# The first 512 tokens by two transposing loads instead of turns on TensorE

## The chip, the cores and the metric

One core of one Trainium2 chip runs the kernel. The metric is the device time of one execution in microseconds (us). A profiled execution gives, beside its own time, the trace that the views below are taken from; times inside it count from the start of its span.

## The reference

The input x has 2048 tokens of 512 numbers in bfloat16. Two branches are computed from it and mixed token by token with a gate:

```python
def reference(A_x, A_wqkv, A_w_phi, A_wo, B_x, B_w1, B_w2, gate_w):
    x = A_x
    g = _sigmoid((x * gate_w).sum(-1, keepdims=True))
    a = _A_ref(x, A_wqkv, A_w_phi, A_wo)   # linear attention, 32 heads of 16
    b = _B_ref(x, B_w1, B_w2)              # relu(x @ w1) @ w2, 1376 hidden
    return g * a + (1 - g) * b
```

In the attention branch q and k of each head go through w_phi (16 x 16), then softmax of the result and of its negative give 32 features; keys and values are summed into one 32 x 16 matrix per head, the queries are multiplied with it and divided by their sum, and wo closes it. B_x is not used.

## The kernel before

Every operation is a named task in a graph with its engine and its dependencies. The order of each engine's tasks is written out by hand in the table ORDER (L17 to L62): one string each for SyncE (`sp`), GpSimd (`pool`), ScalarE (`act`), VectorE (`dve`) and TensorE (`pe`). `emit` puts the tasks on the engine in that order, with a wait for each dependency on another engine or on a load, so an engine stands still when its next task's wait is not over. The numbers `dur`, `lat` and `boost` of a task do not reach the program.

The products need x with its 512 features on the partitions, in the buffer XT: four blocks of 128 features, 2048 tokens wide. x comes in four chunks of 512 tokens. Chunks 1 to 3 (`x1`, `x2`, `x3`) and the weights of K and Q (`wkT`, `wqT`) are loaded by transposing DMAs of SyncE's queue, all issued at L277. Chunk 0 goes another way. Four plain loads of 128 tokens (`x00` to `x03`, L272) bring it into XN, which lies in a buffer of FT; TensorE multiplies each block of 128 x 128 with an identity, IDN, (`xt00` to `xt31`, L350, 16 matmuls), and ScalarE (`xe*0`, L362) and VectorE (`xe*1`, L365) copy the results from PSUM to XT. IDN is made on VectorE (L320) from two iotas of GpSimd.

W1 (512 x 1376) is loaded in parts: its first 512 columns as four blocks of 128 rows (`w1a0` to `w1a3`, alternately on SyncE's and ScalarE's queue), then columns 512 to 1023 (`w1b`) and the rest (`w1c`). Tasks `h{c}_{k}` compute tile k of 128 hidden columns for chunk c, in four matmuls of 512 columns (L391). For chunk 0 the first four tiles are cut up: `hh00`, `hh01`, `hh1`, `hh2`, `hh3` (L405) do the first 256 tokens, W1's row block by row block into four PSUM banks, and `hr0`, `hr1`, `h0_0` to `h0_3` (L411) the other 256 tokens. `h0_4` is the first task at L391. Next come `h0_5`, then the folds `f1_0` to `f1_3` (L374), which multiply K's transposed weights with w_phi (block-diagonal in WBD, made by VectorE from the load `wphi`), and the K projections `pr_k0` on (L512). In front of all is `warm0` (L258): matmuls of 512 columns on constants of one, whose result is not used.

The x turns and the first products stand in the order "warm0 xt00 xt01 xt10 xt11 hh00 hh01 hh1 hh2 xt20 xt21 xt30 xt31 hh3 hr0 hr1 h0_0 ..." on TensorE. SyncE begins with "x00 w1a0 w1a2 x02 x03 w1b wphi wkT w1c wv x1 x2 wqT x3" and ScalarE with "x01 w1a1 w1a3 xe00 xe10 xe20 xe30 rl0_0"; `x1` waits on SyncE for `w1c` to land. `rl{c}_{k}` are ScalarE's relu copies (L469).

Later stages: softmax on ScalarE, VectorE and GpSimd (L539 to L589), the sum over keys (L573), the queries (L616 to L625), W2 and wo (L638, L644), and the stores.

Of the kernel before, what the change touches and what calls it, by code (L numbers as in the profile page):

```python
# [18 lines left out]
        "x00 w1a0 w1a2 x02 x03 w1b wphi wkT w1c wv x1 x2 wqT x3 gw w2a w2b wo hx0 hx1 hx2 tq0 tq1 "  # L19
# [4 lines left out]
        "iota_r iota_i iota_c ones hpad t1_k0 t2_k0 t1_k1 t2_k1 t2_k2 t1_k2 t1_k3 t2_k3 nm_k0 nm_k1 t1_k5 t1_k4 t2_k4 "  # L24
# [5 lines left out]
        "x01 w1a1 w1a3 xe00 xe10 xe20 xe30 rl0_0 rl0_1 rl0_3 rl0_2 rl0_4 fe1_1 fe1_3 rl0_5 ev_k0 rl0_8 rl0_6 "  # L30
# [9 lines left out]
        "ident shift xe01 xe11 xe21 xe31 blk row4 wbd1 wbd3 mk wbd2 wbd0 fe1_0 fe1_2 mx_k0 mn_k0 mx_k1 mn_k1 "  # L40
# [11 lines left out]
        "warm0 xt00 xt01 xt10 xt11 hh00 hh01 hh1 hh2 xt20 xt21 xt30 xt31 hh3 hr0 hr1 h0_0 h0_1 h0_2 h0_3 h0_4 "  # L52
# [96 lines left out]
def bass_gated_mix__linear_kernel_hedgehog__dense_activation_relu__prompt_kernel(  # L149
# [34 lines left out]
    WARM = (6 * (512,),)  # L184
# [3 lines left out]
    with ExitStack() as es:  # L188
        E = es.enter_context

        def sb(name, shape, dt):
            return E(nc.sbuf_tensor(name, shape, dt))
# [28 lines left out]
        COLI = sb("COLI", [P, P], I32)  # L221
        IDN = sb("IDN", [P, P], BF16)
# [23 lines left out]
        add("iota_i", "pool", lambda q: q.iota(COLI[:, :], [[1, P]], channel_multiplier=0), dur=0.25, boost=800.0)  # L246
# [5 lines left out]
        XN = FT[:, NF - 2, :].rearrange("p (m d) -> p m d", d=D)  # L252
# [32 lines left out]
        x0r = x2[chunk(0), :].rearrange("(m p) d -> p m d", p=P)  # L285
        wvr = A_wqkv[:, 2 * D:3 * D].rearrange("(j p) n -> p j n", p=P)
        def load_x(m, eng, lat):
            load(f"x0{m}", eng, XN[:, m, :], x0r[:, m, :], dur=0.45, lat=lat)

        def load_w(j, eng, lat):  # L290
            load(f"w1a{j}", eng, W1[:, j, 0:512], w1r[:, j, 0:512], dur=0.45, lat=lat)

        load_x(0, "sp", 2.95)
        load_x(1, "act", 3.1)
        load_w(0, "sp", 3.2)
        load_w(1, "act", 3.4)
        load_w(2, "sp", 3.8)
        load_w(3, "act", 3.95)
        load_x(2, "sp", 4.0)
        load_x(3, "sp", 3.9)  # L300
# [5 lines left out]
        g.follow("iota_r", "iota_i")  # L306
        g.follow("iota_i", "iota_c")
# [12 lines left out]
        add("ident", "dve", lambda q: q.tensor_tensor(IDN[:, :], ROWH[:, :], COLI[:, :], ALU.is_equal),  # L320
            ("iota_r", "iota_i"), dur=0.3, boost=2000.0)
# [13 lines left out]
        def pe_turn(q, b, blocks):  # L335
            for n, src in enumerate(blocks):
                last = q.matmul(PS[:, b, n * P:(n + 1) * P], src, IDN[:, :], start=True, stop=True)
            return last

# [6 lines left out]
        XB, FB = ((0, 1), (6, 7), (0, 1), (6, 7)), (0, 1, 6, 7)  # L346

        def pe_xt(q, m, n):
            for j in range(2 * n, 2 * n + 2):
                last = q.matmul(PS[:, XB[m][j // 2], (j % 2) * P:(j % 2 + 1) * P], XN[:, m, j * P:(j + 1) * P],  # L350
                                IDN[:, :], start=True, stop=True)
            return last

        for m in range(4):
            for n in range(2):
                add(f"xt{m}{n}", "pe", lambda q, m=m, n=n: pe_xt(q, m, n),
                    (f"x0{m}", "ident", f"xe{m - 2}{n}" if m > 1 else None), dur=0.2, boost=9000.0 - 10 * m)
            for n, eng in enumerate(("act", "dve")):
                xo = XT[:, 2 * n:2 * n + 2, m * P:(m + 1) * P]
                xi = PS[:, XB[m][n], 0:2 * P].rearrange("p (j t) -> p j t", j=2)  # L360
                if eng == "act":
                    add(f"xe{m}{n}", eng, lambda q, o=xo, i=xi: q.activation(o, i, ACT.Copy), (f"xt{m}{n}",), dur=0.35,  # L362
                        boost=9000.0 - 10 * m)
                else:
                    add(f"xe{m}{n}", eng, lambda q, o=xo, i=xi: q.tensor_copy(o, i), (f"xt{m}{n}",), dur=0.37,  # L365
                        boost=9000.0 - 10 * m)
        x0 = [f"xe{m}{n}" for m in range(4) for n in range(2)]
# [18 lines left out]
        freed[FB[2]] = ("xe30",)  # L386
# [30 lines left out]
        add("hh00", "pe", lambda q: pe_h_first(q, 0, 0, P), ("xe00", "w1a0"), dur=0.22, boost=8500.0)  # L417
        add("hh01", "pe", lambda q: pe_h_first(q, 0, P, 2 * P), ("xe10", "hh00"), dur=0.22, boost=8500.0)
        prev = "hh01"
        for j in range(1, ND):  # L420
            add(f"hh{j}", "pe", lambda q, j=j: pe_h_first(q, j, 0, 2 * P), (f"xe0{j // 2}", f"xe1{j // 2}", f"w1a{j}", prev), dur=0.44,
                boost=8500.0)
            prev = f"hh{j}"

        for k in range(2):
            add(f"hr{k}", "pe", lambda q, k=k: pe_h_rest(q, k, 2 * P, 3 * P, True), ("xe20", "xe21", prev), dur=0.22,
                boost=8200.0)
            prev = f"hr{k}"
        for line in (("warm0", "xt00", "xt01", "xt10", "xt11", "hh00", "hh01", "hh1", "hh2", "xt20", "xt21", "xt30", "xt31",
                      "hh3", "hr0", "hr1"), ("xe00", "xe10", "xe20", "xe30"),  # L430
                     ("ident", "shift", "xe01", "xe11", "xe21", "xe31", "blk", "row4", "mk")):
            for a, b in zip(line, line[1:]):
                g.follow(a, b)
# [8 lines left out]
        for n, (kind, a, k) in enumerate(units):  # L442
            b = GB4[n] if n < 4 else FB[2] if n == 4 else HB[(n - 4) % len(HB)]
            if kind == "h":
                halved = n < 4
                deps = [*xof[a], *w1of[k], prev, *freed[b]]
                if k == KT - 1:
                    deps.append("gw")
                    add(f"h{a}_{k}", "pe", lambda q, a=a, b=b: pe_h_tail(q, a, b), deps, dur=0.69)
                    prev = f"h{a}_{k}"  # L450
                    hrow = psap(b * 512, [[KREM + 1, 4], [1, KREM]])
                    add(f"rl{a}_{k}", "act", lambda q, a=a, i=hrow: q.activation(
                        HR[:, a % 2, :, 0:KREM], i, ACT.Relu), (prev, f"hx{a - 2}" if a > 1 else None), dur=0.6, boost=RL)
                    add(f"hx{a}", "sp", lambda q, a=a: q.dma_start_transpose(
                        out=HT[:, KT - 1, chunk(a)].rearrange("p (n t) -> p n t", t=P),
                        in_=HR[:, a % 2, :, :].rearrange("p n k -> p (n k)")),
                        (f"rl{a}_{k}", "hpad"), dur=1.2, lat=1.6, dma=True)
                    add(f"gr{a}", "dve", lambda q, a=a, b=b: q.tensor_scalar(
                        GL[:, 4 * a:4 * a + 4], psap(b * 512 + KREM, [[KREM + 1, 4]]), GATE_LIMIT, -GATE_LIMIT,
                        ALU.min, ALU.max), (prev, f"rl{a}_{k}"), dur=0.2, boost=500.0)  # L460
                    freed[b] = (f"rl{a}_{k}", f"gr{a}")
                    gate(a)
                    continue
                add(f"h{a}_{k}", "pe", lambda q, a=a, k=k, b=b, h=halved:
                    pe_h_rest(q, k, (3 if k < 2 else 2) * P, 4 * P, k > 1) if h else pe_h(q, a, k, b),
                    deps, dur=(0.22 if k < 2 else 0.44) if halved else 0.87,
                    boost=8000.0 if n < 3 else 0.0)
                prev = f"h{a}_{k}"
                add(f"rl{a}_{k}", "act", lambda q, a=a, k=k, b=b: q.activation(  # L469
                    HT[:, k, chunk(a)], PS[:, b, :], ACT.Relu), (prev,), dur=0.6, boost=RL)  # L470
                freed[b] = (f"rl{a}_{k}",)
            else:
                deps = ["wqT", *wbd, prev, *freed[b]]
                add(f"f{a}_{k}", "pe", lambda q, a=a, k=k, b=b: pe_fold(q, a, k, b), deps, dur=0.24, boost=1000.0)
                prev = f"f{a}_{k}"
                evict(f"fe{a}_{k}", FE, WP[:, a, k, :], b, (prev,), boost=1000.0)
                freed[b] = (f"fe{a}_{k}",)


        for j in range(ND):  # L480
            b = FB[j]
            war = [f"xe{2 + j // 2}{j % 2}"] + (["rl0_4"] if j == 2 else [])
            add(f"f1_{j}", "pe", lambda q, j=j, b=b: pe_fold(q, 1, j, b), ("wkT", *wbd, *war), dur=0.24,
                boost=1800.0)
            evict(f"fe1_{j}", ("dve", "act")[j % 2], WP[:, 1, j, :], b, (f"f1_{j}",), boost=1800.0)
# [31 lines left out]
        for jn, (kind, tiles) in enumerate(jobs):  # L517
# [37 lines left out]
            if jn == NF - 2:  # L555
                war += [f"xt{m}{n}" for m in range(4) for n in range(2)]
# [181 lines left out]
```

## Time and profile before

| | us |
|---|---|
| median of three runs | 150.18 |
| the three runs | 150.1, 150.18, 150.44 |
| the profiled execution, its own time | 150.59 |
| its span, first to last instruction | 149.3 |
| around the span | 1.29 |
| TensorE busy (1009 matmuls) | 146.3 |
| VectorE, ScalarE, GpSimd busy | 110.9, 91.8, 109.6 |
| DMA | 16.11 MB, 108 GB/s on average |

How to read it: PE is TensorE's matmuls, PEld its weight loads, DVE is VectorE, ACT ScalarE, POOL GpSimd, SP SyncE; SPq and ACTq are issues of loads on these engines' queues. Matmuls overlap one another, so the duration of one is longer than the distance to the next. L12 is line 12 of the kernel. In the chain each piece has its start and its length in us, the engine, what it writes, the line and the number of instructions; in the timeline, start, length, engine, line, operation, out<-in, shape, count and the idle time in front. The list of DMA issues has out<-in, the queue, the kind, the count, the size, and the median time from the issue to the landing.

### The profile page before, as it was taken

Reading aid. Unit: us, or ns where it says so; the run is one execution under the profiler, and the core shown is the slowest. Engines: PE = TensorE matmul, PEld = TensorE weight load, DVE = VectorE, ACT = ScalarE, POOL = GpSimd, SP = SyncE. Lnnn points to the kernel's source line nnn. Section 1 sums busy time; section 2 is a strip of 40 time slices with the busy share of each in tenths; the row PEclk is TensorE's granted clock in tenths of the full one; section 3 lists DMA queues with packets and bytes.
Section 4 is the critical chain, followed back from the end, with each engine's and each line's share of the span. In section 5 each row is a group of like instructions: output and inputs, shape, how many; then the busy total and the mean of one; then the engine's idle time right before and its main releaser. Section 6 shows DMA issues by size and latency. Waiting matters only on the chain.

```text
span 149.3 us, 2619 instructions
## 1 busy us (share of the span) xinstructions
PE 146.3 (98%) x1009; PEld 75.9 (51%) x1009; DVE 110.9 (74%) x168; ACT 91.8 (61%) x127; POOL 109.6 (73%) x72
## 2 busy tenths in 40 slices
PE   7999999999999999999999999999999999999994
PEld 2865444444754465445444545455444444445452
DVE  2343666999796948989999997999989988534401
ACT  3374769799979775898983937175573751310151
POOL 4000399999999999999999999999999793150000
PEclk9999999999999999999999999999999999999999
DMA  5999999900030001000000094646778687656552
GB/s 144 303 234 247 171 212 211 341 27 0 7 70 0 0 4 37 0 0 4 0 0 0 2 111 104 141 103 139 121 169 190 159 212 97 156 134 159 63 156 91
DMA packets 46364, 16.11 MB, mean 108 GB/s; under 512 B 39856, under 2 KB 46352, under 8 KB 46352
## 3 DMA queue, kind: packets, MB, share of 16 engines
q1 hardware_dynamic: 43616, 13.50, 43.2%
q10 hardware_dynamic: 2736, 2.45, 5.1%
q8 instruction: 8, 0.13, 0.4%
q14 instruction: 4, 0.03, 0.1%
HBM read 4.41 MB, written 2.10 MB: 44 GB/s over the span
## 4 chain that ended last, share of the span: by engine, by line
PE 98%; DVE 0%; issue 0%
PE PS L638 24%; PE PS L391 21%; PE PS L512 19%; PE PS L492 9%; PE PS L644 9%; PE PS L573 3%; PE PS L616 3%; PE PS L399 2%; PE PS L405 2%; PE PS L258 2%; PE PS L659 2%; PE PS L411 1%; PE PS L374 1%; PE PS L350 1%; PE PS L670 1%; DVE OSB L680 0%
## 5 line engine op out<-in xcount | busy, mean ns | idle before, releaser
L552 POOL TENSOR_TENSOR TS<-PB,MX 128x1024 bf16<-128x1024 bf16 (+1 forms) x18 | 30.9, 1723 | 15.0 <-DVE MX L543 15.0
L638 PE MATMUL PS<-W,HT 128*128 128x512 bf16 (+1 forms) x165 | 38.1, 379 | 0.0
L559 DVE TENSOR_REDUCE ZB<-FT 128x128 f32<-128x2048 bf16 (+1 forms) x18 | 36.6, 2031 | 1.8 <-ACT FT L557 1.8
L557 ACT ACTIVATE FT<-TS 128x2048 bf16<-128x2048 bf16 (+1 forms) x18 | 30.9, 1718 | 8.7 <-POOL TS L552 8.5
L391 PE MATMUL PS<-XT,W 128*128 128x512 bf16 x144 | 34.7, 379 | 0.0
L552 POOL TENSOR_TENSOR TS<-MN,PB 128x1024 bf16<-128x1024 bf16 (+1 forms) x18 | 30.9, 1725 | 0.8 <-DVE MN L545 0.8
L512 PE MATMUL PS<-WP,XT 128*128 128x512 bf16 x128 | 30.6, 379 | 0.0
L566 POOL TENSOR_TENSOR FT<-FT,SC 128x2048 bf16<-128x2048 bf16 (+1 forms) x9 | 29.5, 3287 | 0.0
L469 ACT ACTIVATE HT<-PS 128x512 bf16<-128x512 f32 x40 | 22.6, 597 | 5.6 <-PE PS L391 4.6
L638 PEld LDWEIGHTS PS<-W,HT 128*128 128x128 bf16 (+1 forms) x165 | 15.5, 98 | 17.1
L689 ACT ACTIVATE OSB<-PS,OMG 128x512 bf16<-128x512 f32 x15 | 10.2, 687 | 22.4 <-PE PS L644 22.3
L543 DVE TENSOR_REDUCE MX<-PB 128x64 bf16<-128x1024 bf16 (+1 forms) x18 | 19.5, 1084 | 6.0 <-ACT PB L539 6.0
L545 DVE TENSOR_REDUCE MN<-PB 128x64 bf16<-128x1024 bf16 (+1 forms) x18 | 19.3, 1084 | 3.2 <-ACT PB L539 3.2
L391 PEld LDWEIGHTS PS<-XT,W 128*128 128x128 bf16 x144 | 13.8, 98 | 15.3
L539 ACT ACTIVATE PB<-PS 128x1024 bf16<-128x1024 f32 (+1 forms) x18 | 16.7, 927 | 7.3 <-PE PS L512 4.2
L512 PEld LDWEIGHTS PS<-WP,XT 128*128 128x128 bf16 x128 | 12.0, 98 | 13.6 <-DVE WP L344 0.4
L492 PE MATMUL PS<-WV,XT 128*128 128x512 bf16 x64 | 16.4, 379 | 0.0
L589 POOL TENSOR_TENSOR FT<-FT,SR 128x1024 bf16<-128x1024 bf16 (+1 forms) x9 | 15.7, 1739 | 0.7
L644 PE MATMUL PS<-WO,OT 128*128 128x512 bf16 x60 | 14.7, 379 | 0.0
L625 DVE SCALAR_TENSOR_TENSOR OTM<-PS,EG,RD 128x256 bf16<-128x256 f32 x32 | 13.8, 463 | 0.4 <-DVE RD L623 0.2
L623 DVE RECIPROCAL RD<-PS 128x16 f32<-128x16 f32 x32 | 6.4, 232 | 9.0 <-PE PS L616 8.8
L501 ACT ACTIVATE VS<-PS 128x512 bf16<-128x512 f32 x16 | 9.6, 602 | 4.3 <-PE PS L492 4.3
(54 smaller groups left out, 106.0 us busy)
## 6 DMA issues: line engine op xcount, KB each, us to landing
out_dram<-OSB ACTq DMA_DIRECT2D x15, 128.0 KB, 2.1
W<-in_B_w_dram SPq DMA_DIRECT2D x1, 1280.0 KB, 6.9
W<-in_B_w_dram SPq DMA_DIRECT2D x1, 512.0 KB, 4.9
WV<-in_A_wqkv_dram SPq DMA_DIRECT2D x1, 512.0 KB, 4.7
WO<-in_A_wo_dram SPq DMA_DIRECT2D x1, 512.0 KB, 7.2
FT<-in_A_x_dram SPq DMA_DIRECT2D x3, 128.0 KB, 3.8
W<-in_B_w_dram SPq DMA_DIRECT2D x1, 352.0 KB, 3.9
W<-in_B_w_dram ACTq DMA_DIRECT2D x2, 128.0 KB, 3.7
```

The source lines that it names most:

```text
L391: last = q.matmul(PS[:, b, :], W1[:, j, k * P:(k + 1) * P], XT[:, j, chunk(c)], start=(j == 0), stop=(j == ND - 1))
L469: add(f"rl{a}_{k}", "act", lambda q, a=a, k=k, b=b: q.activation(HT[:, k, chunk(a)], PS[:, b, :], ACT.Relu), (prev,), dur=0.6, boost=RL)
L492: last = q.matmul(PS[:, 2, :], XT[:, j, m * P:(m + 1) * P], WV[:, j, :], start=(j == 0), stop=(j == ND - 1))
L512: last = q.matmul(PS[:, n, :], XT[:, j, m * P:(m + 1) * P], WP[:, s, j, :], start=(j == 0), stop=(j == ND - 1))
L543: add(f"mx_{J}", "dve", lambda q, sl=sl, w=w, i=pbg: q.tensor_reduce(MX[:, sl, 0:w * H], i, AX.X, ALU.max), (f"ev_{J}", old("t1")), dur=0. ...
L545: add(f"mn_{J}", "dve", lambda q, sl=sl, w=w, i=pbg: q.tensor_reduce(MN[:, sl, 0:w * H], i, AX.X, ALU.min), (f"ev_{J}", old("t2")), dur=0. ...
L552: add(f"{tn}_{J}", "pool", lambda q, o3=o3, a3=a3, b3=b3: q.tensor_tensor(o3, a3, b3, ALU.subtract), (f"{'mx' if sg == 0 else 'mn'}_{J}", ...
L557: add(f"ex_{J}", "act", lambda q, fs=fs, ts=ts, w=w: q.activation(FT[:, fs, 0:w * F], TS[:, ts, 0:w * F], ACT.Exp), (f"t1_{J}", f"t2_{J}", ...
L559: add(f"sm_{J}", "dve", lambda q, fs=fs, sl=sl, w=w: q.tensor_reduce(ZB[:, sl, 0:2 * w * H], FT[:, fs, 0:w * F].rearrange("p (g d) -> p g ...
L566: add(f"nm_{J}", "pool", lambda q, f3=f3, sl=sl, w=w: q.tensor_tensor(f3, f3, SC[:, sl, 0:2 * w * H].unsqueeze(2).to_broadcast([P, 2 * w * ...
L638: last = q.matmul(PS[:, ab, :], HT[0:r, k, m * P:(m + 1) * P], W2[0:r, k, :], start=(k == 0), stop=False)
L644: last = q.matmul(PS[:, ab, :], OT[:, m % NOT, t, :], WO[:, t, :], start=False, stop=(t == ND - 1))
```

## The change

Chunk 0 is loaded like the others, by transposing DMAs, but in two halves of 256 tokens: `x0a` and `x0b`, first on SyncE's queue, straight into XT. All four row blocks of W1's first 512 columns are issued on ScalarE's queue, one after the other. The 16 turns, the eight copies of their results, IDN, one iota and XN fall away. `hh0` to `hh3` are now four alike, 4 matmuls of 256 columns each, which wait for `x0a` and for their block of W1. `h0_0` to `h0_3` each do the other 256 tokens in 4 matmuls of 256 columns, and `h0_0` waits for `x0b`. `warm0` has seven matmuls in place of six. From `h0_4` on all orders are as before.

```diff
 ORDER = {
     "sp": (
-        "x00 w1a0 w1a2 x02 x03 w1b wphi wkT w1c wv x1 x2 wqT x3 gw w2a w2b wo hx0 hx1 hx2 tq0 tq1 "
+        "x0a x0b w1b wphi wkT w1c wv x1 x2 wqT x3 gw w2a w2b wo hx0 hx1 hx2 tq0 tq1 "
...
     "act": (
-        "x01 w1a1 w1a3 xe00 xe10 xe20 xe30 rl0_0 rl0_1 rl0_3 rl0_2 rl0_4 fe1_1 fe1_3 rl0_5 ev_k0 rl0_8 rl0_6 "
+        "w1a0 w1a1 w1a2 w1a3 rl0_0 rl0_1 rl0_3 rl0_2 rl0_4 fe1_1 fe1_3 rl0_5 ev_k0 rl0_8 rl0_6 "
...
     "dve": (
-        "ident shift xe01 xe11 xe21 xe31 blk row4 wbd1 wbd3 mk wbd2 wbd0 fe1_0 fe1_2 mx_k0 mn_k0 mx_k1 mn_k1 "
+        "shift blk row4 wbd1 wbd3 mk wbd2 wbd0 fe1_0 fe1_2 mx_k0 mn_k0 mx_k1 mn_k1 "
...
     "pe": (
-        "warm0 xt00 xt01 xt10 xt11 hh00 hh01 hh1 hh2 xt20 xt21 xt30 xt31 hh3 hr0 hr1 h0_0 h0_1 h0_2 h0_3 h0_4 "
+        "warm0 hh0 hh1 hh2 hh3 h0_0 h0_1 h0_2 h0_3 h0_4 "
...
-    WARM = (6 * (512,),)
+    WARM = (7 * (512,),)
...
-        load_x(0, "sp", 2.95)
-        load_x(1, "act", 3.1)
-        load_w(0, "sp", 3.2)
-        load_w(1, "act", 3.4)
-        load_w(2, "sp", 3.8)
-        load_w(3, "act", 3.95)
-        load_x(2, "sp", 4.0)
-        load_x(3, "sp", 3.9)
+        for n in range(2):
+            load_t(f"x0{'ab'[n]}", XT[:, :, n * 2 * P:(n + 1) * 2 * P], x2[n * 2 * P:(n + 1) * 2 * P, :], (), 1.3, 2.0)
+        for j in range(ND):
+            load(f"w1a{j}", "act", W1[:, j, 0:512], w1r[:, j, 0:512], dur=0.45, lat=3.0)
...
-        add("hh00", "pe", lambda q: pe_h_first(q, 0, 0, P), ("xe00", "w1a0"), dur=0.22, boost=8500.0)
-        add("hh01", "pe", lambda q: pe_h_first(q, 0, P, 2 * P), ("xe10", "hh00"), dur=0.22, boost=8500.0)
-        prev = "hh01"
-        for j in range(1, ND):
-            add(f"hh{j}", "pe", lambda q, j=j: pe_h_first(q, j, 0, 2 * P), (f"xe0{j // 2}", f"xe1{j // 2}", f"w1a{j}", prev), dur=0.44,
-                boost=8500.0)
+        prev = "warm0"
+        for j in range(ND):
+            add(f"hh{j}", "pe", lambda q, j=j: pe_h_first(q, j, 0, 2 * P), ("x0a", f"w1a{j}", prev), dur=0.44, boost=8500.0)
             prev = f"hh{j}"
 
-        for k in range(2):
-            add(f"hr{k}", "pe", lambda q, k=k: pe_h_rest(q, k, 2 * P, 3 * P, True), ("xe20", "xe21", prev), dur=0.22,
-                boost=8200.0)
-            prev = f"hr{k}"
...
-                    pe_h_rest(q, k, (3 if k < 2 else 2) * P, 4 * P, k > 1) if h else pe_h(q, a, k, b),
-                    deps, dur=(0.22 if k < 2 else 0.44) if halved else 0.87,
+                    pe_h_rest(q, k, 2 * P, 4 * P, True) if h else pe_h(q, a, k, b),
+                    deps, dur=0.44 if halved else 0.87,
```

## The prediction

> **What bounds the kernel now.** I read the page's busy shares first, then the chain of waits in order of time, then the start of the timeline for TensorE's weight loads and for SyncE's queue, and last the matmuls by shape on both sides of 6.4 us. Shares and clock:
>
> ```profile
> PE 146.3 (98%) x1009; PEld 75.9 (51%) x1009; DVE 110.9 (74%) x168; ACT 91.8 (61%) x127; POOL 109.6 (73%) x72
> PEclk9999999999999999999999999999999999999999
> ```
>
> TensorE is busy for 98% of the span, and the chain that ends last is TensorE from its first instruction on. So what counts is when its long stream begins, and how fast it runs at first. The chain's first pieces (start, length, what):
>
> ```profile
> 0.77 2.72 PE PS L258 x6
> 3.49 0.99 PE PS L350 x8
> 4.48 2.33 PE PS L405 x16
> 6.81 0.45 PE PS L350 x8
> 7.25 0.44 PE PS L405 x4
> 7.69 1.88 PE PS L411 x24
> 9.57 1.73 PE PS L391 x8
> ```
>
> Six warm matmuls, eight turns, then the first products with W1. The same eight turns cost 0.99 us at 3.49 and 0.45 us at 6.81: TensorE runs at half speed first, although the page's clock row shows 9 from its first slice. Starts of the warm weight loads in the timeline:
>
> ```profile
> 1.16 0.15 PEld L258 LDWEIGHTS PS<-const-bfloat16-1.0 128*128 128x128 bf16 x1 [0.28 <-issue]
> 1.58 0.15 PEld L258 LDWEIGHTS PS<-const-bfloat16-1.0 128*128 128x128 bf16 x1 [0.28 <-issue]
> ```
>
> The groups by shape, for 256-column matmuls before 6.4 us (first line) and after 6.45 us (second; columns: count | busy us, mean ns of one | idle):
>
> ```profile
> L405 PE MATMUL PS<-XT,W 128*128 128x256 bf16 x6 | 1.4, 414 | 0.0
> ...
> L411 PE MATMUL PS<-XT,W 128*128 128x256 bf16 x8 | 1.0, 272 | 0.0
> ```
>
> At half speed 512 columns follow each other every 0.425 us, so 256 columns every 0.213. At full speed the chain has 0.44/4 = 0.11 us (I use 0.109) for 256 columns. The step comes at 6.4 us, which is 5.63 us after the first matmul at 0.77, in a stream with no stop longer than about 0.15 us (the sixth warm matmul gives way at 0.77 + 6 x 0.425 = 3.3, the first turn starts at 3.44).
>
> The mark I count to is h0_4, the first matmul of L391, at 9.40 us in the timeline. Behind it the view of waits has nothing over 0.4 us for TensorE, and all that other engines feed it starts from its own products, so a shift of h0_4 goes through to the end one for one.
>
> **The change, part by part.** *Removed from TensorE*: 16 turns of 128 columns, 0.99 us at half and 0.45 us at full speed, and a stop of 0.2 us before L411. *Unchanged*: the first products, now 32 matmuls of 256 columns (16 in hh0 to hh3, 16 in h0_0 to h0_3). *Removed elsewhere, at nothing*: four ScalarE copies (0.81 and 0.66 us in two pairs), four VectorE copies, the identity and an iota; all lay beside TensorE's turns and products. The iota, the identity and the shift on VectorE were done before x landed.
>
> *Added, a seventh warm matmul*: 0.425 us, ending at 0.77 + 7 x 0.425 = 3.75 us. It delays nothing if x lands later.
>
> *Added, the two transposing loads.* They are first on SyncE's queue. That queue in the timeline of before:
>
> ```profile
> 0.74 0.40 SPq L272 DMA_DIRECT2D FT<-in_A_x_dram  x1
> ...
> 3.08 0.43 SPq L272 DMA_DIRECT2D W<-in_B_w_dram  x1
> ...
> 19.41 2.40 SPq L277 DMA_TRANSPOSE XT<-in_A_x_dram  x1
> ```
>
> and from the page's list of issues (count, median us to landing):
>
> ```profile
> PHQ<-FT SPq DMA_TRANSPOSE x16, 2.9
> ...
> XT<-in_A_x_dram SPq DMA_TRANSPOSE x3, 5.5
> ```
>
> x0a is 256 rows of 512, 256 KB: the bytes of a PHQ transpose (2.9 us to landing, but out of SBUF) and half those of an x load (5.5 us, 5.7 at most, out of HBM, some of it behind other loads). Bounds: 0.74 + 2.9 = 3.65 and 0.74 + 5.7 = 6.4 us. The bytes decide more than the source, so I start from 3.65 and add what W1's blocks on ScalarE's queue take from the same transfers: 256 KB of them in the meantime, at the 318 GB/s that the windows view shows for 3.4 to 6.4 us, 0.8 us. **x0a lands at 4.5 us.** W1's first block needs about 2.9 us from issue on either queue, 3.6 us, so x0a is what hh0 waits for (d_x0a and d_w1a0 are its two waits), and behind hh0 stands all of TensorE. x0b is issued about 1.25 us after x0a (half of 2.40 to 2.52) and lands near 5.8; h0_0 needs it 16 matmuls after hh0, at 7.2 even with the clock full from 6.4.
>
> *Moved past on SyncE's queue*: x0a and x0b take 2.5 us of issue where five loads took 2.3, so W1's second part, the w_phi load, K's transposed weights and all behind start 0.2 us later. Landings before: W1's second part 3.08 + 4.9 = 8.0 for a use at 9.40; K's weights 4.12 + 5.8 = 9.9 for 11.13; x1 11.80 + 5.5 = 17.3 for 19.0. Slack 1.2 us at least: nothing, unless h0_4 comes over 1 us earlier. On ScalarE's queue a fourth issue (0.4 us) pushes the table load from 2.15 to 2.6, ending at 3.9; its first eviction is after 8 us.
>
> *The stop.* From 3.75 to 4.5 us TensorE has nothing: 0.75 us, where before it had 0.15. What a stop inside the half-speed stretch does to the step at 6.4 is not in this trace. Bounds: the step stays at 6.4; or the count begins anew at 4.5 and takes the 5.63 us that the trace shows from idle, to 10.13. Between them, were only the dense stream after 3.44 counted, 4.5 + 2.96 = 7.46. In 32 matmuls to h0_4:
> - step at 6.4: 8.9 at 0.213, 23.1 x 0.109 = 2.52, h0_4 at 8.92, -0.48 us.
> - step at 7.46: 13.9, then 18.1 x 0.109 = 1.97, h0_4 at 9.43, +0.03 us.
> - step at 10.13: 26.4, then 5.6 x 0.109 = 0.61, h0_4 at 10.74, **+1.34 us**.
>
> I take the last: the only full record of how the clock rises from idle is 5.63 us, and the warm stream alone (0.77 to 3.75, 2.98 us) is shorter than anything that raised it. The Trainium skill, "TensorE: Matmul & The Clock Gate", Part 1 (the warmup mystery), says that the array starts at half clock and is released after one busy window of about 3.4 us, in windows that run free of the kernel's start; the trace agrees so far, since 5.63 lies between one and two such windows. By that rule, with a stop spoiling its window, an estimate is a step between 7.9 and 11.3, h0_4 near 10.5, about +1.1 us.
>
> The profiled execution took 150.59 (span 149.3 and 1.29 around it), 0.41 over the median of 150.18. The sum is a difference, so 150.59 becomes 151.93, and the median 150.18 + 1.34 = 151.5.
>
> **The rivals.**
> 1. *The clock doesn't mind the stop* (faster). Step at 6.4 as before, 0.48 us gained: 149.7. For it: 0.15 us of stop did no harm, and TensorE is still busy for most of the time before 6.4. Against: 0.75 us is five times that. It decides by x0a's landing: at 3.9 us hardly a stop is left and the gain is 0.8 (149.4); with the step fixed, each us of later landing costs 0.49, and the gain is gone at 5.5 us. What may bring x0a early is the 2.9 us row; what may make it late is the 5.5 us row.
> 2. *The count pauses and goes on* (no change). The step moves by the extra stop of 0.6 to 0.75 us, to about 7.15: 12.4 matmuls slow, 19.6 x 0.109 = 2.14, h0_4 at 9.3, 150.1. Nothing in the profile speaks for or against a pause.
> 3. *The loads become the bound with the clock intact* (slower). If the transposing loads share badly with W1's four blocks, x0a lands at 5.9 or later, or W1's second part slips from 8.2 to over 9.6: h0_4 at 9.65, 150.4 and up. For it: the transposed load of K's weights took 3.72 us to issue with 0.5 MB in front of it, where 2.4 is usual. Against: nothing is in front of x0a. This is also how the change could fail at its aim, to start the products without TensorE's own turns. The same skill, "DMA: Bandwidth & Descriptors", in "Issuing engines are not separate DMA queues", says that loads from two queues interleave on the same 16 engines and only issue time is saved; the windows view agrees, with a DMA share over 1 from 3.4 us on.
>
> **How the numbers follow.** Forecast (count begins anew) 0.56, rival 1 0.31, rival 2 0.07, rival 3 0.06. Forecast's own range: x0a at 4.0 to 5.0 us moves it by a quarter us each way, a step 1.2 us earlier takes off 0.55: 150.9 to 151.9. Cases of both signs hold most of the chance, so the range for 8 in 10 reaches to rival 1: 149.5 to 151.9. About 0.2%, 0.3 us, is what the runs can tell from no change (three of them spread over 0.34). Faster by more: 0.31, nearly all of rival 1 and some of its early landings. Within: rival 2 and a rival 1 with x0a near 5 us, 0.09. Slower: 0.60.
>
> **What would show it.** In the profile after: the first product of 256 columns at the timeline's 4.5 us, a stop on TensorE of 0.75 us before it, released by the load of XT. The mean of the hh and h0_0 to h0_3 matmuls: near 414 ns for about 26 of 32 (forecast), or 272 for some 23 of 32 (rival 1). Start of the first 512-column product: 10.7, 8.9, 9.3 or past 9.6. The rest of the chain one unbroken TensorE stream, with POOL's first subtraction moved from 17.29 by the same amount. I am wrong if the half-speed stretch ends at 6.4 again, if x0a lands before 3.9, or if TensorE shows a new wait for W1's second part or K's weights.

## The result and the profile after

The changed kernel took 151.86 us as the median of five runs (151.41 to 153.28), the kernel before 150.18 us (150.03 to 150.85, six runs): 1.0112 times as long, with an interval of 1.0073 to 1.0152, or 1.7 us more. Medians, spreads and ratios here and below leave out runs in the slow state, those more than 1.5% above the fastest of the same kernel (here one of 153.82). The forecast was 151.5 us in a range of 149.5 to 151.9, so the direction is right, the size 0.36 us short, and the median just inside the range's upper end. The profiled execution is one of the longer ones: 153.28 us, with a span of 151.9 us (149.3 before).

The page's busy shares, clock row and shares of the chain after the change:

```profile
PE 146.3 (96%) x965; PEld 75.3 (50%) x982; DVE 109.0 (72%) x163; ACT 90.5 (60%) x123; POOL 109.4 (72%) x71
...
PEclk9999999999999999999999999999999999999999
...
PE 92%; DMA 4%; ACTq 1%; issue 1%; DVE 0%
```

TensorE is busy for the same 146.3 us, although the turns are gone; the span grew by 2.6 us, and 4% of the chain now is DMA. The chain in order of time (start, length, what) names the load:

```profile
2.12 6.23 DMA W<-in_B_w_dram
8.36 0.05 issue
8.40 1.03 PE PS L362 x4
9.44 2.95 PE PS L368 x16
```

L254, L362, L368 and L348 are the lines 258, 405, 411 and 391 of before. W1's fourth block, issued by ScalarE at 2.12, lands at 8.36; it landed at 5.89 before. TensorE's timeline (start, length, what, count, idle before and what ended it) shows both stops:

```profile
0.77 3.14 PE L254 MATMUL PS<-const-bfloat16-1.0 128*128 128x512 bf16 x7 [0.77 <-PEq L669]
4.75 2.74 PE L362 MATMUL PS<-XT,W 128*128 128x256 bf16 x12 [0.83 <-DMA XT<-in_A_x_dram]
8.40 1.03 PE L362 MATMUL PS<-XT,W 128*128 128x256 bf16 x4 [0.91 <-DMA W<-in_B_w_dram]
9.23 3.15 PE L368 MATMUL PS<-XT,W 128*128 128x256 bf16 x16
12.22 1.89 PE L348 MATMUL PS<-XT,W 128*128 128x512 bf16 x8
```

The first stop, 0.83 us for x0a, was forecast as 0.75. The second, 0.91 us before hh3, was not forecast: it waits for W1's fourth block. The first 512-column product, the mark of the prediction, starts at 12.22 (9.40 before): 2.82 us later, of which 2.6 arrive at the end of the span. TensorE goes to full speed only at 11.76 (until then its matmuls follow each other at 0.213 us for 256 columns, afterwards at 0.109).

Why the block is late stands in the view of windows, as a table by stage; its last columns are the granted clock, the DMA engines' share and the GB/s that they moved. (The granted clock of 1.00 doesn't show the half-speed stretch; that is read from the distances of the matmuls and from where the trace's clock record begins.) Before, then after, from 4.5 to 8.0 us:

```profile
4.50:8.00 3.50, 3.50 (x35) 2.81 (x34) 1.37 (x6) 0.84 (x3) 0.00 (x0) 1.00 1.15 294
```

```profile
4.50:8.00 3.50, 2.74 (x12) 1.65 (x12) 0.00 (x0) 0.00 (x0) 0.00 (x0) 1.00 1.18 158
```

The DMA engines are as occupied as before (1.15 and 1.18) and move half as much (294 and 158 GB/s). From 2.0 to 4.5 us it was still 284 and 267. Only the second transposing load, x0b, and what is queued with it falls into the slow stretch: x0b lands at 8.59, W1's second part at 9.89 (7.98 before), K's weights at 11.80 (9.92 before).

### The profile page after: what moved, and what is told of

The parts are those of the page before. It is cut to its first block, busy times and chain, and to the rows that moved or that the text cites. A ratio compares the mean times of both kernels' runs of the same rounds, so it can differ in the third digit from the quotient of the medians.

```text
span 151.9 us, 2532 instructions
## 1 busy us (share of the span) xinstructions
PE 146.3 (96%) x965; PEld 75.3 (50%) x982; DVE 109.0 (72%) x163; ACT 90.5 (60%) x123; POOL 109.4 (72%) x71
## 4 chain that ended last, share of the span: by engine, by line
PE 92%; DMA 4%; ACTq 1%; issue 1%; DVE 0%
PE PS L584 23%; PE PS L348 20%; PE PS L460 18%; PE PS L440 9%; PE PS L590 8%; DMA W<-in_B_w_dram 4%; PE PS L519 3%; PE PS L562 3%; PE PS L368 2%; PE PS L356 2%; PE PS L605 2%; PE PS L331 1%; ACTq L268 1%; PE PS L362 1%; PE PS L616 1%
## 5 line engine op out<-in xcount | busy, mean ns | idle before, releaser
L584 PE MATMUL PS<-W,HT 128*128 128x512 bf16 (+1 forms) x160 | 37.5, 379 | 0.3
L348 PE MATMUL PS<-XT,W 128*128 128x512 bf16 x140 | 34.3, 379 | 0.2
L460 PE MATMUL PS<-WP,XT 128*128 128x512 bf16 x125 | 30.1, 379 | 0.2
L348 PEld LDWEIGHTS PS<-XT,W 128*128 128x128 bf16 x144 | 13.8, 98 | 15.3
L440 PE MATMUL PS<-WV,XT 128*128 128x512 bf16 x61 | 15.8, 379 | 0.2
L590 PE MATMUL PS<-WO,OT 128*128 128x512 bf16 x58 | 14.2, 378 | 0.1
```

Source lines behind the costliest of these rows:

```text
L348: last = q.matmul(PS[:, b, :], W1[:, j, k * P:(k + 1) * P], XT[:, j, chunk(c)], start=(j == 0), stop=(j == ND - 1))
L440: last = q.matmul(PS[:, 2, :], XT[:, j, m * P:(m + 1) * P], WV[:, j, :], start=(j == 0), stop=(j == ND - 1))
L460: last = q.matmul(PS[:, n, :], XT[:, j, m * P:(m + 1) * P], WP[:, s, j, :], start=(j == 0), stop=(j == ND - 1))
L584: last = q.matmul(PS[:, ab, :], HT[0:r, k, m * P:(m + 1) * P], W2[0:r, k, :], start=(k == 0), stop=False)
L590: last = q.matmul(PS[:, ab, :], OT[:, m % NOT, t, :], WO[:, t, :], start=False, stop=(t == ND - 1))
```

## The experiments

Two theories had to be told apart. **The clock**: what costs the time is the half-speed stretch, made longer by TensorE's stop for x0a. **The loads**: what costs it is that packets of a transposing load in flight beside W1's plain blocks bring the transfer rate down, whatever the clock does. Beside the loads stood cheaper explanations of the same late block: that W1's blocks were all put on one queue, that x now comes in small pieces, or that K's transposing load gets in the way.

Measured times are medians; a ratio is against runs of the kernel before on the same chip, whose median was 150.33 us for the first four experiments, 150.45 for the next four and 150.53 for the last four. "The mark" is the start of the first 512-column product.

The time around the span, the run's time less its span, has a median of 1.3 to 1.4 us in the kernel before, in the changed one and in five of the variants. In the other six (the queues of the change in the kernel before, the two with one queue, both queues, plain loads in small pieces, half of the change) it is 1.6 to 1.7 us. What makes the difference isn't known; about 0.3 us of the excess of these six lies outside the span.

**The changed kernel once more.** No edit.

> The changed kernel once more, unaltered, to see what of its first 12 us comes back. In its first profile x0a landed at 4.7 us, W1's fourth row block at 8.4, x0b at 8.6, and the half-speed stretch ended after 11 us. Theory 'clock' (the stop on TensorE before hh0 makes the half-speed stretch begin anew): the products run at half speed well past 6.4 us again, and the median is 1.3 us or more over before. Rival 'data' (the late landings of W1's fourth block and x0b set the start, the clock is secondary): both land after 8 us again, and the first 512-column product stands within 0.5 us of where 16 full-speed matmuls after that landing would put it, 10.5 us. Third possibility, chance: the landings differ by over 1 us from the first profile, and the time with them.

Measured: 151.75 us (151.16 to 152.09), ratio 1.0089 [1.0064, 1.0114]; profiled 152.09, span 150.7. TensorE's timeline:

```profile
4.80 2.74 PE L362 MATMUL PS<-XT,W 128*128 128x256 bf16 x12 [0.89 <-DMA XT<-in_A_x_dram]
8.84 0.61 PE L362 MATMUL PS<-XT,W 128*128 128x256 bf16 x4 [1.29 <-DMA W<-in_B_w_dram]
9.28 1.91 PE L368 MATMUL PS<-XT,W 128*128 128x256 bf16 x16
```

Both stops are back, the second even longer, and W1's fourth block lands at 8.79. But here full speed comes at 8.23, not 11.76: the sixteen matmuls of L368 take 1.91 us instead of 3.15, and the mark is at 11.03. So the late block belongs to the change, and the moment of full speed varies from execution to execution.

**Ten warm matmuls**, to fill the stop for x0a and take the clock out of the question.

```diff
-    WARM = (7 * (512,),)
+    WARM = (10 * (512,),)
```

> The changed kernel with ten warm matmuls in place of seven, which end at about 5.0 us, behind the landing of x0a (4.7). Nothing else differs. Clock theory: no stop any more before hh0, so the half-speed stretch ends at 7.6 us at the latest, and what is left is the late W1 block and x0b: first 512-column product at about 10.6 us, time about 151.3, some 0.7 to 1.5 under the changed kernel. Data theory: the products wait for W1's fourth block and x0b as before, hh0 starts 0.3 us later and nothing is gained: 152.0.

Measured: 151.47 us (151.38 to 151.77), 1.0078 [1.0059, 1.0098]; profiled 151.46, span 150.2.

```profile
5.82 1.48 PE L362 MATMUL PS<-XT,W 128*128 128x256 bf16 x12 [1.22 <-DMA XT<-in_A_x_dram]
8.31 0.61 PE L362 MATMUL PS<-XT,W 128*128 128x256 bf16 x4 [1.00 <-DMA W<-in_B_w_dram]
```

x0a came late in this execution (5.77), so a stop was left; but full speed came at 3.86, earlier than before's 6.42, and every product runs at it. The mark is still at 10.50, 1.10 us later than before, because hh3 still waits for W1's fourth block at 8.26. Mark and time are near those of the clock theory (10.6 and 151.3), which left the late block in. That is the loads' part: 0.0078 x 150.33 = 1.17 us. The clock's part on average is what the changed kernel has above it, 0.0034 or 0.0011 of 150 us, 0.5 or 0.2 us; the intervals overlap. In single executions it differs. In the first profile of the changed kernel the mark is 12.22 - 10.50 = 1.7 us later than here, and W1's fourth block only 0.1 us: nearly all of that is the clock. In the second it is 11.03 - 10.50 = 0.53 us later, and the block just as much (8.79 against 8.26): there the clock took nothing at the mark. The narrow spread (0.4 us, against 1.9 and 0.9 us in the two series of the changed kernel) fits that the part that varies was the clock's.

**The kernel before with four warm matmuls**: a stop of about the same size in a kernel without the new loads.

```diff
-    WARM = (6 * (512,),)
+    WARM = (4 * (512,),)
```

> The kernel before with four warm matmuls in place of six: they end at 2.5 us, and TensorE stops for 0.95 us until the first turn at 3.44. All loads and all else as before. Clock theory (a stop makes the count begin anew): the half-speed stretch ends between 6.9 and 10.3 us and not at 6.4, the first 512-column product is later by half of the difference, 0.2 to 1.9 us, 151.2 in the middle. If the count only pauses: +0.45 us, 150.6. If a stop does nothing: 150.2, no change.

Measured: 150.93 us (149.77 to 151.64, twelve runs), 1.0035 [1.0011, 1.0059]. TensorE's timeline:

```profile
3.33 1.04 PE L350 MATMUL PS<-IDN,FT 128*128 128x128 bf16 x8 [0.69 <-DMA FT<-in_A_x_dram]
```

A stop of 0.69 us, full speed at 6.90 (6.42 before), the mark at 9.58. The step does not come 5.63 us after the stop, which would be 8.96. On average the stop costs 0.0035 x 150.33 = 0.5 us, and the spread widens from 1.0 to 1.9 us, which fits a price that differs from execution to execution.

**x0b only after W1's fourth block**: x0b's issue waits until W1's blocks have landed, so that they share with x0a alone.

```diff
-            load_t(f"x0{'ab'[n]}", ..., (), 1.3, 2.0)
+            load_t(f"x0{'ab'[n]}", ..., ("w1a3",) if n else (), 1.3, 2.0)
```

> The changed kernel in which x0b waits on SyncE until W1's fourth row block has landed; everything behind it on that queue waits too. If x0b's transposing packets hold up W1's blocks, the fourth lands near 5.3 us instead of 8.4, and x0b some 3.2 us after its issue, near 8.5. If W1's blocks are late for another reason (fourth on their queue, memory slow at the start), the fourth lands after 7 us still. The time is not the point here: with the loads behind x0b some 3 us later it should be slower than the changed kernel or equal to it, 152 to 154; the half-speed stretch begins anew with the stop before hh0 as in the changed kernel.

Measured: 153.27 us (152.8 to 153.41), 1.0190 [1.0164, 1.0216]. TensorE's timeline:

```profile
4.70 3.60 PE L363 MATMUL PS<-XT,W 128*128 128x256 bf16 x16 [0.78 <-DMA XT<-in_A_x_dram]
8.61 2.45 PE L369 MATMUL PS<-XT,W 128*128 128x256 bf16 x16 [0.31 <-DMA XT<-in_A_x_dram]
11.31 1.04 PE L349 MATMUL PS<-XT,W 128*128 128x512 bf16 x4 [0.26 <-DMA W<-in_B_w_dram]
```

With x0b and what is behind it on SyncE's queue out of the way, W1's fourth block lands at 5.53, earlier than before's 5.89, and hh0 to hh3 are one stream of 16 matmuls. So W1's four blocks get on well beside x0a in this execution. The price is paid elsewhere: x0b is issued at 5.55 and lands at 8.56, and W1's second part behind it at 11.27, which is now a wait. This alone doesn't say whether it was x0b or W1's second part that held up the fourth block; the plain loads below do.

**The queues of the change in the kernel before**: the four pieces of x on SyncE's queue, W1's four blocks on ScalarE's, all plain.

```diff
-        "x00 w1a0 w1a2 x02 x03 w1b wphi ...
+        "x00 x01 x02 x03 w1b wphi ...
-        "x01 w1a1 w1a3 xe00 ...
+        "w1a0 w1a1 w1a2 w1a3 xe00 ...
```

> The kernel before with the queues of the change and nothing else of it: four plain loads of x on SyncE's queue, W1's four row blocks on ScalarE's, turns on TensorE as before. Theory 'mix' (transposing packets beside plain ones on the other queue slow both): without transposing packets W1's fourth block lands near 6 us, as x03 and W1's last block did before (5.9 to 6.4), and the time is within 0.4 us of before, about 150.4. Rival 'order' (fourth place on one queue is what makes it late): it lands after 8 us, and the time is 151 or more.

Measured: 150.69 us (150.36 to 151.35, ten runs), 1.0021 [1.0006, 1.0037]. W1's fourth block lands at 6.33, the last piece of x at 6.15, and 275 GB/s move from 4.5 to 8.0. The division among the queues costs 0.4 us of landing, not 2.5. Full speed comes at 5.14 in the profiled execution and the mark at 8.86, yet the time isn't better than before's. The profiled execution is the fastest of the ten; their median span is 149.1 us against 149.0 of the kernel before on that chip, and around it lie 1.60 us against 1.34.

**One queue for all**, in two orders, with ten warm matmuls as in all that follow but the last: x0a, x0b, then W1's blocks on SyncE's queue; or x0a, W1's blocks, then x0b.

```diff
-        "x0a x0b w1b wphi ...
+        "x0a x0b w1a0 w1a1 w1a2 w1a3 w1b wphi ...      (the first)
+        "x0a w1a0 w1a1 w1a2 w1a3 x0b w1b wphi ...      (the second)
-        "w1a0 w1a1 w1a2 w1a3 rl0_0 ...
+        "rl0_0 ...
```

> The changed kernel with ten warm matmuls and all of it on SyncE's queue, in the order x0a, x0b, W1's four row blocks; ScalarE issues no load. Mix theory: alone on the engines the transposing loads go at the pace of the later ones, x0a lands near 3.7 us and x0b near 4.9, W1's fourth block near 7.3, over 1 us sooner than beside each other, though all six are issued from one queue. If the engines are simply full (rival 'volume': 1 MB needs that long in any order), the last of the six lands at 8.3 or later again. Time: about 151.0 by the first (last landing 7.3, then 7 or 8 matmuls at full speed, W1's second part next), 151.5 by the second.

> As the last one, in the order x0a, W1's four row blocks, x0b. Mix theory: x0a near 3.7 us, W1's fourth block near 5.6, x0b near 7; TensorE starts with W1's first block near 4.3 and has its products up to x0b done by about 6.5 to 7.5, first 512-column product at about 8.8 to 9.2, limited by W1's second part near 9: time 149.8 to 150.2, at or below the kernel before. Volume rival: x0b lands at 8.5, first 512-column product at 10.3, 151.3.

Measured: 152.83 us (152.38 to 152.91), 1.0149 [1.0125, 1.0173], and 152.25 us (152.06 to 152.52), 1.0119 [1.0099, 1.0138]. TensorE's timeline of the first:

```profile
6.25 2.12 PE L365 MATMUL PS<-XT,W 128*128 128x256 bf16 x16 [1.11 <-DMA W<-in_B_w_dram]
...
10.78 1.90 PE L351 MATMUL PS<-XT,W 128*128 128x512 bf16 x8 [0.66 <-DMA W<-in_B_w_dram]
```

Transposing loads with nothing in front of them and no other queue beside them are quick: x0a lands at 4.15 and x0b at 5.28 in the first, x0a at 3.89 in the second, which is the earliest of all kernels. The last of the six loads lands at 7.71 and 7.58, before the 8.6 of the changed kernel. But W1's second part, next on the same queue, lands at 10.73 and 10.39 and is now waited for (0.66 and 0.89 us). It isn't slow itself: it is issued only at 5.51 and 5.45 (3.08 before), behind six loads on the one queue, and lands 5.2 and 4.9 us later (4.9 before). The landings of the six came within 1 us of what the mix theory expected and before those of its rival; both times missed the expectation, by 1.8 and over 2 us.

**Both queues, x0b last of the six**: W1's first two blocks on ScalarE's queue, x0a, the other two and x0b on SyncE's.

```diff
+        "x0a w1a2 w1a3 x0b w1b wphi ...     (SyncE)
+        "w1a0 w1a1 rl0_0 ...                (ScalarE)
```

> The changed kernel with ten warm matmuls, W1's first two row blocks on ScalarE's queue, and on SyncE's x0a, W1's third and fourth block, x0b. Mix theory: x0a is disturbed by the first two blocks and lands near 4.6, after that only one kind is in flight at a time: W1's fourth block near 5.5, x0b near 6.8, first 512-column product 8.7 to 9.1, time 149.7 to 150.1. Volume rival: x0b at 8.5 or later, 151.3.

Measured: 151.77 us (150.86 to 152.38), 1.0084 [1.0056, 1.0112]; the profiled execution is the fastest, 150.86, span 149.2. In it W1's fourth block lands at 6.21, x0b at 7.02, the mark is at 9.07 and full speed at 3.96: the start that the change was meant to have. Still the span isn't shorter than before's 149.3, and the median is 0.9 us above the profile. TensorE stops for 0.92 us before hh0, at 5.57, and for 0.17 us at 11.13 for K's weights. That the slower runs had a later step of the clock fits the spread and is not shown: no profile of them was taken. This one missed its expectation.

**Plain loads in small pieces**: the first 512 tokens by four plain loads of 128 tokens in pieces of 256 bytes, into the same places. x of these tokens isn't transposed here, so the products are computed from other numbers, at the same shapes.

```diff
-            load_t(f"x0{'ab'[n]}", XT[:, :, n * 2 * P:(n + 1) * 2 * P], x2[n * 2 * P:(n + 1) * 2 * P, :], (), 1.3, 2.0)
+        for m in range(4):
+            load(f"x0{'aabb'[m]}{m % 2}", "sp", XT[:, :, m * P:(m + 1) * P], x2[m * P:(m + 1) * P, :].rearrange(...), ...)
```

> As the last one, but with plain loads in pieces of 256 B, as large as the transposing loads' packets, four loads of 128 tokens (x is again not transposed). If the small pieces are the cause, not the transposing itself, x0b and W1's fourth block land past 8 us and the time is near 151.4. If it is the transposing, the fourth block lands before 7 us and the time is below 150.3.

Measured: 150.99 us (150.52 to 151.21, eight runs), 1.0037 [1.0016, 1.0059]; span of the profiled execution 148.9. Windows view, first of the kernel with ten warm matmuls above, then of this one; then TensorE's timeline of this one:

```profile
4.50:8.00 3.50, 1.59 (x13) 1.09 (x12) 0.00 (x0) 0.00 (x0) 0.00 (x0) 1.00 1.18 208
...
4.50:8.00 3.50, 3.50 (x25) 2.39 (x24) 0.00 (x0) 0.09 (x1) 0.00 (x0) 1.00 1.07 273
```

```profile
5.15 2.29 PE L363 MATMUL PS<-XT,W 128*128 128x256 bf16 x16
7.28 1.91 PE L369 MATMUL PS<-XT,W 128*128 128x256 bf16 x16
9.02 1.89 PE L349 MATMUL PS<-XT,W 128*128 128x512 bf16 x8
```

This experiment says most about the loads. Same bytes, same small packets, same queues, W1's second part issued at 3.47 as in the changed kernel (3.46): only the transposing of x is gone (and x comes in four issues instead of two), and the rate is 273 GB/s instead of 158 (208 with ten warm matmuls), W1's fourth block lands at 6.02 instead of 8.36, x0b's two halves by 7.09 instead of 8.59, and the second stop is gone. The single packets in the trace agree: W1's packets of 1024 bytes on ScalarE's queue that started between 4.5 and 8.0 us took 141 and 136 ns on average in the two profiles of the changed kernel, 98 with ten warm matmuls, and 48 here. In spans, the median excess over the kernel before falls from 1.2 us with ten warm matmuls (150.2 against 149.0) to 0.25 (149.35 against 149.1); the rest of this kernel's excess lies around the span.

It shows a second thing too: even with the loads mended the mark is at 9.02, only 0.38 us before that of the kernel with the turns, and the median is above before's and above the 150.3 that was expected. K's weights land at 10.84, about where they are first used (10.89).

**Plain loads in larger pieces**, 512 bytes, two loads of 256 tokens, on the same queue; again x isn't transposed.

> The variant with ten warm matmuls in which x0a and x0b are plain loads of the same 256 KB each, in pieces of 512 B, in place of transposing ones: x of the first 512 tokens is not transposed, everything else is as in that variant. If the transposing loads are what makes W1's row blocks late (mix), x0a lands near 4.3 us, W1's fourth block and x0b near 6.3, W1's second part near 8.0 as before, first 512-column product at 8.0 to 8.6 us, time 149.1 to 149.8, below the kernel before. If two queues with 1 MB at the start are what is slow, the fourth block lands after 8 us again and the time is 151.4.

Measured: 151.6 us (151.6 to 152.0), 1.0087 [1.0061, 1.0114]. The profiled execution is another one, of 154.0, with a stretch of half speed from 8.95 to 12.37 that came back after full speed at 5.54; its marks are not compared. W1's fourth block landed at 8.80 although 283 GB/s moved from 4.5 to 8.0 and x0b was there at 6.61. So a fourth block can be late without a loss of rate. Here its packets weren't slow (46 ns on average, against 141) and the last of them had ended by 7.2; the landing was told 1.6 us later. K's transposing load, whose issue lasted here from 3.34 to 8.55, was in flight then, with single packets of 256 bytes that took up to 1.25 us; whether it held up the landing was not isolated, and this expectation was missed.

**K's weights later**: the transposing load of K's weights moved behind the third part of W1 and V's weights; ten warm matmuls.

```diff
-        "x0a x0b w1b wphi wkT w1c wv x1 ...
+        "x0a x0b w1b wphi w1c wv wkT x1 ...
```

> The variant with ten warm matmuls, with the transposing load of K's weights moved behind W1's third part and V's weights on SyncE's queue. In the kernels where W1's fourth block was late, this load was being issued (from 4.6 us on) while x0b and W1's blocks were in flight; where x0b waited, it was not. If its issue is what slows them, W1's fourth block and x0b land before 7 us now. If x0b's own packets beside W1's do it, both land near 8.2 again. The time is worse in both cases, 153 to 156, since the folds wait for K's weights.

Measured: 154.37 us (153.91 to 154.88), 1.0263 [1.0231, 1.0296]. Windows view:

```profile
4.50:8.00 3.50, 2.09 (x14) 1.01 (x12) 0.00 (x0) 0.00 (x0) 0.00 (x0) 1.00 1.20 163
```

K's load is issued at 6.83 instead of 4.62, W1's fourth block lands at 8.66 all the same, and the rate is 163 GB/s. So in the changed kernel it isn't K's load that holds up the block. K's weights themselves land at 15.02 and cost the rest.

**Half of the change**: the turns stay for the first 256 tokens, and only x0b is a transposing load, fourth on SyncE's queue. Six warm matmuls.

```diff
-        "x00 w1a0 w1a2 x02 x03 w1b ...
+        "x00 w1a0 w1a2 x0b w1b ...
-        "... hh2 xt20 xt21 xt30 xt31 hh3 hr0 hr1 h0_0 ...
+        "... hh2 hh3 h0_0 ...
```

> One part of the change alone: the first 256 tokens by plain loads and turns on TensorE as before, the other 256 by one transposing load, fourth on SyncE's queue, in place of two plain ones. Six warm matmuls. It saves 8 turns (0.45 us) and four copies. Mix theory: W1's last two blocks are in flight beside x0b, so x0b lands near 7.5 us and W1's second part near 9, the first 512-column product at 9.3 to 9.7, time 150.3 to 150.7, no gain. If a transposing load behind plain ones on its queue is harmless, x0b lands near 6.5, W1's second part at 8.3, the product stands at 8.8 and the time is 149.8.

Measured: 150.70 us (150.09 to 151.05, twelve runs), 1.0017 [1.0002, 1.0032]. TensorE's timeline:

```profile
8.84 1.90 PE L390 MATMUL PS<-XT,W 128*128 128x512 bf16 x8 [0.29 <-DMA W<-in_B_w_dram]
10.92 1.07 PE L373 MATMUL PS<-WBD,WT 128*128 128x128 bf16 x16 [0.18 <-DMA WT<-in_A_wqkv_dram]
```

W1's fourth block lands at 5.69 and x0b at 6.59, so nothing is late there. That is against the mix theory, which had x0b at 7.5, and for its rival, by which a transposing load behind plain ones on its queue is harmless; full speed came at 3.57 in this execution. The mark moves forward by 0.56 us to 8.84 and is then held by W1's second part (8.79), and the folds by K's weights (10.87, against 9.92 before): they start at 10.92, 0.21 us before those of the kernel with all turns. Over all runs nothing is left of that: the median span is 149.1 us as in the kernel before, and with 1.62 us around it instead of 1.32 the time is 0.2 to 0.3 us longer, at the edge of what can be told.

No version beat the kernel before.

## Why the prediction was right in its direction and wrong in its reason

- **x0a at 4.5 us**: right, 4.71 and 4.76. Bounding it between the 2.9 us and the 5.5 us row and leaning to the nearer in bytes worked. It is not a constant, though: 5.03, 5.53 and 5.77 were seen with the same load first on the queue.
- **The stop of 0.75 us**: right, 0.83 and 0.89.
- **x0b "near 5.8"**: here the step failed that the sum rests on, the overlap of the loads. It took half of an issue time as the distance between the landings and so assumed that x0b transfers as fast as x0a. It landed at 8.59 and 8.97. The 318 GB/s was read where plain loads were in flight, from 3.4 to 6.4 us; in the same stretch the mixture ran at 198 and 176, and from 4.5 to 8.0 at 158 and 136.
- **W1's blocks**: the same step, and the one that cost the time. Only the first was costed ("3.6 us"), because hh0 waits for it. The other three are each a wait of hh1 to hh3, one place further back on the queue; the forecast put them at nothing without a reason, and the fourth, at 8.36 and 8.79, became the second stop of 0.91 and 1.29 us. "Every landing that a moved product waits for" would have been the list to make. None of the three signs of being wrong showed either: they asked for a new wait for W1's second part or K's weights, not for its first part.
- **Later loads, "slack 1.2 us at least: nothing"**: W1's second part lands 1.9 us later instead of 0.2, K's weights too. No wait came of it in the changed kernel, only because the mark itself had slipped by more.
- **The clock, "the count begins anew" for 5.63 us**: wrong as a rule. Full speed should have come at 10.13; it came at 11.76 once and at 8.23 the other time, the latter 3.4 us after hh0 began; counted from the end of the second stop it would be past 14 in both. The "count pauses" of rival 2 gives 7.15 and falls too. That the step at 6.4 would be missed held in both profiles.
- **+1.34 us**: the sum came out near what was measured, 1.7 us by the ratio (0.0112 x 150.2) and 1.3 the second time (0.0089 x 150.3), by an exchange of causes, and that is luck. The loads give about 1.2, for which the forecast had nothing, and the clock 0.2 to 0.5 on average, for which it had all.
- **One for one to the end**: right within 0.2 us: +2.82 at the mark gave +2.6 of span, +1.63 gave +1.4.
- **The edits costed at nothing** (copies, identity, iota): no wait came of them.
- **Rival 1** (149.7) had one condition, the clock, and took the loads as free. With the clock at full speed from 3.86 on, ahead of all 6.4, the ten-warm kernel still has its mark at 10.50 and not at 8.92.
- **Rival 3** had the mechanism, "the transposing loads share badly with W1's four blocks", and 0.06. Its places were wrong (x0a and W1's second part, not x0b and the fourth block), and the argument against it, that nothing is in front of x0a, speaks for x0a alone. Its own row, K's transposing load that took 3.72 us to issue with 0.5 MB in front of it, pointed the same way, and weighed little.

## What to carry to other kernels

When a load changes its kind, cost anew every landing that shares the time with it, not only its own: a rate taken from plain loads need not hold for plain and transposing ones together. Then list each product's own wait, block by block, because the last of four loads sets the stop and not the first. And take turns off TensorE at the start of a kernel only if the data allow an earlier start: here even loads that shared well brought the mark forward by 0.4 us. The turns had stood in part where TensorE would have waited for weights: with half of the change it stood for 0.27 us, until 5.62, for W1's third block.

## What the runs showed of the hardware that was not expected

**Transposing beside plain loads.** From 4.5 to 8.0 us the rate was 136 to 163 GB/s in the two profiles of the changed kernel and with K's load moved (208 with ten warm matmuls, 246 where x0b alone was a transposing load, 286 with both queues, where x0b came behind W1's blocks), against 268 to 294 in the five profiles with plain loads of the same bytes, at about the same DMA share (1.10 to 1.21, and 1.07 to 1.27). The Trainium skill, "Advanced Engine Details and Errata", section X-Bar Transpose (TRN2), says that transposing DMAs are as fast as regular ones. For one without another queue beside it the runs don't contradict it (x0a, 256 KB, lands at 3.89 and 4.15 on one queue, 3.2 and 3.4 us after its issue begins at 0.74; W1's plain blocks of half the bytes have a median of 2.6 and 2.7 us there); beside plain loads the measurement decides, and in the kernels with both transposing loads in front the rate is half to three quarters. Why x0a's own stretch, from 2.0 to 4.5 us, still ran at 267 GB/s and x0b's didn't is open. It isn't always so: with ten warm matmuls x0a's stretch ran at 212 GB/s, and x0a landed at 5.77. Nor is every mixture slow: x0b alone behind plain loads (246) and x0b behind W1's blocks (286) came close to the plain ones. The slow profiles are those with both transposing loads first on SyncE's queue and W1's four blocks beside them on ScalarE's; what in that makes them slow wasn't isolated.

**When TensorE goes to full speed.** The long full-speed stretches in the trace's clock record last 139.95, 143.36 or 146.77 us, which are 41, 42 and 43 times 3.413 us. So the decision seems to fall at the ends of fixed windows of that length, whose place differs from execution to execution. For each window of 3.41 us, the share of it in which columns streamed (at half speed 512 columns take 0.425 us, 1.2 columns per ns), the last before the step and the one before that:

| kernel, profiled execution | full speed from | last window | window before it |
|---|---|---|---|
| before | 6.42 us | 0.93 | 0.65 |
| before, four warm | 6.90 us | 0.98 | 0.53 |
| after | 11.76 us | 0.98 | 0.69 (and 0.70 before that) |
| after, second time | 8.23 us | 0.74 | 0.68 |
| half of the change | 3.57 us | 0.77 | no work yet |

In the eleven profiles whose record has the step, every window of 0.74 and more raised the clock, and none of 0.70 and less did; five are shown. That would explain the two profiles of the changed kernel: the same stops cut two windows to 0.69 and 0.70 in one, and left 0.74 in the other, 3.5 us earlier. The Trainium skill, "TensorE: Matmul & The Clock Gate", Part 1, has such windows of 3413 ns that run free of the kernel's start, and the trace agrees with the length; the share that a window needs, here between 0.70 and 0.74, it doesn't give. The share is worked out from these profiles and was not tested by a run of its own. In the kernel with plain loads of 512 bytes one window with a stop of 2.1 us was followed by half speed again, from 8.95 to 12.37; with ten warm matmuls a window with a stop of 1.2 us at full speed was not.
